# Seven products of halves inside the real part: the product P2 of two blocks of a Strassen kernel made as inner products

## The chip, the cores and the metric

The kernel runs on one core of one Trainium2 chip. The time is the device time of one execution in microseconds; the kernel before takes 701.67 us in the median of three runs (701.47 to 701.92). Five engines run beside each other: TensorE (PE, with its weight loads PEld), VectorE (DVE), ScalarE (ACT), GpSimd (POOL) and SyncE (SP). Here the last two only issue DMAs: SP the loads, POOL the stores and the DMAs that add to their destination.

## The reference

Inputs are x (2048 x 512), DFT matrices over the sequence (2048 x 2048, real and imaginary) and over the hidden axis (512 x 512, the same), the weights w1, w3 (512 x 1376) and w2 (1376 x 512), and a gate vector (512). What is computed:

```
g = sigmoid((x * gate_w).sum(-1))
a = x @ dft_hid_re.T ;  b = x @ dft_hid_im.T
A = dft_seq_re @ a - dft_seq_im @ b
h = silu(x @ w1) * (x @ w3)
out = g * A + (1 - g) * (h @ w2)
```

All is float32. The kernel reaches that precision by splitting each operand into a rounded high part and the rest, a low part, and making three matmuls of each product: high by high, high by low, low by high.

## The kernel before, in words

The work comes in three stages on TensorE. First the hidden DFT (tiles dP), whose results a and b go to DRAM (`ab`). Then gate and up (tiles X, Y, Z), eleven chunks of 128 columns, whose product h goes to DRAM (`hsp`). Then six blocks of large products, each with 512 output rows and 1024 columns: `BLOCKS` numbers them b = 0 to 5, with m = 0 for h @ w2 (b 0, 1), m = 1 for the real part (b 2, 3) and m = 2 for the imaginary part (b 4, 5). j = 0 or 1 is the half of the 2048 columns.

Each block is one product of 2 x 2 submatrices made in Strassen's way (Winograd's form) as seven products P1 to P7. The stationary operand comes from `ab` or w2 in forms of A11, A12, A21, A22; the moving operand from the sequence matrix (`cc`) or h, in forms of B11, B12, B21, B22: F1 = B11+B12, F2 = F1+B22, F3 = B12+B22, F4 = F2+B21. P2 is A12 x B21.

**Steps.** `STEPS` is the list of all work of TensorE in this stage, in order; `AT` gives the place of a step. One step is one product with one quarter of the inner dimension: 12 matmuls of 128x512. `step(n)` makes the matmuls, then calls `advance(n)`, then the tasks hung at that step (`TASKS`), and, where a product is complete, takes the result out of PSUM. `advance(n)` loads the raw blocks of steps up to 8 ahead (`load_c`, tiles B), sums the form of the step 4 ahead (`sum_c`, line 658, on VectorE) and splits that of the step 3 ahead (`split_c` through `split`, lines 71 and 74: ScalarE makes the high part zh, VectorE the low part zl). These tiles stand in a pool of 8 (`zo`), four steps' worth.

**Forms of A.** The stationary forms are made ahead. `forms(m, q, ks, keep)` loads the rows of one quarter and makes the products' forms `ks` in place in the order given by `IN_PLACE` (`sum_a`, lines 481 to 488), splits each (lines 71, 74) and either stores it to DRAM (`fsp`, line 514) or keeps it (`keep`). It returns a list of pieces. The pieces of gate and up are put into one list, `later`, and `work(count)` takes some from it at hooks h0 to h4 of each chunk (`item`). Kept forms are made as tasks during the blocks. `load_a` loads stored ones back (tiles a0, a1, a2). Kept and loaded forms share 28 buffers (`op`). Raw blocks, weights of gate and up (`load_w`, line 249), raw rows, forms under way to DRAM and results share 19 buffers (`f4`).

**Inner products.** In the imaginary part P2 of both blocks is not made in steps of its own. Both have the same A12; so their two B21 together are one product of 2 x 2 submatrices, of half the size, and it too is made as seven products. These are the steps whose names begin with L: `inner_step` puts two half steps of 6 matmuls each for every inner product between the outer steps (`BETWEEN` says after which), `inner(n)` runs them in one PSUM tile (Lx), line 831 adds each inner result to the result tile that P1 began, and the inner stationary forms come from `inner_forms` by way of DRAM (`lsp`, `load_inner`, tiles fl and al). The raw inner blocks are tiles LB. In these blocks F4 and two of the inner forms are not summed on VectorE: `add_block` (line 646) issues a DMA on POOL's queue that reads the second block and adds it to the tile in SBUF, behind the split that has read the tile. Block 2 has one such sum too, F3 (`BY_DMA`).

**What sets the order.** The program is written with a framework that places the waits, gives out buffers and orders each engine's instructions by a cost model of its own; loads by `fetch` and the instructions marked `pinned` keep the written order. SP's and POOL's queues issue in order: a load that waits for a buffer holds the loads behind it.

In the diff `LB` holds the blocks with inner products and `INTO` where each inner result goes. `finish` (lines 767 to 797) ends a quarter of a block: for m = 1 it scales and adds only two quarters of block 3 and stores the others as they are (`ysp`); for m = 2 it subtracts, scales and adds to the output.

Of the kernel before, what the change touches and what calls it, by code (L numbers as in the profile page):

```python
# [7 lines left out]
F32 = mybir.dt.float32  # L8
# [4 lines left out]
P = 128  # L13
# [5 lines left out]
NP = (NC - 1) // 2  # L19
NQ = 4  # L20
WARM = 16


HEAD = ((0, 0, 0, 256), ("d", 0, 0, 512), (0, 0, 256, 256), (1, 0, 0, 512), ("d", 1, 0, 512),
# [4 lines left out]
def fnet_swiglu_gate_kernel(  # L29
# [29 lines left out]
    def raw(name, n=1024):  # L59
        return f4.tile([P, n], F32, tag="f4", name=name)  # L60
# [414 lines left out]
    A = {}  # L475
# [54 lines left out]

    def inner_forms():

        st = {}

        def cols(t, v):
            return t.rearrange("p (c h e) -> p c h e", c=4, h=2)[:, :, v]

        def quads(ap):
            return ap.rearrange("p (c e) -> p c e", c=4)

        def load():
            for h in range(2):
                st[h] = raw(f"rl{h}")
                for q in range(2):
                    nc.sync.dma_start(
                        st[h][:, q * 512 : (q + 1) * 512], ab[1, 1, 2 * h + q, :, 0].rearrange("p i e -> p (i e)"))

            st["a11"], st["a21"], st["a12"], st["a22"] = (cols(st[h], v) for h in range(2) for v in range(2))

        def total(k):  # L550
            st[k] = sum_a(st, k)

        def parts(k):
            src = st[k]
            t = f4.tile([P, 2, 512], F32R, tag="f4", name=f"fl{k}")
            split(quads(t[:, 0]), quads(t[:, 1]), src)
            nc.gpsimd.dma_start(lsp[PRODS.index(k)], flat(t.bitcast(F32)))
# [26 lines left out]
    todo = list(INNER)  # L584
# [7 lines left out]
    count, BETWEEN = 0, (4, 5, 7, 8, 10, 11, 13, 14, 17, 19)  # L592
    LORDER = ("P1", "P5", "P6", "P7", "P3", "P4")
    for b, (m, j) in enumerate(BLOCKS):
        for k, form in ((k, FORM[k]) for k in LORDER) if b in LB else CHAIN:
            for q in range(NQS[m]):
                AT[b, k, q] = len(STEPS)
                STEPS.append((b, k, q, form))
                if len(todo) <= 12:
                    if count in BETWEEN:  # L600
                        inner_step()
                    count += 1
            if b in LB and k == "P6":

                for _ in range(2):
                    inner_step()
# [38 lines left out]
    def add_block(t, b, k, q):  # L645
        nc.gpsimd.dma_start(half(t, chunks(b, q)), block(b, k, q), accum_op=ALU.add)

    BY_DMA = (2,)

    def sum_c(n):  # L650
        if not 0 <= n < len(STEPS):
            return
        b, k, q, form = STEPS[n]
        o = {"F1": "B12", "F2": "B22", "F4": "B21", "F3": "B22", "LF2": "LB22", "LF3": "LB22"}.get(form)
        if not o or q == "pl" or form == "F3" and b in BY_DMA or form == "F4" and b in LB:
            return
        t = RAW[b, "L" * (form[0] == "L") + ("B12" if form[-2:] == "F3" else "B11"), q]
        nc.vector.tensor_add(t, t, RAW[b, o, q])  # L658

    def split_c(n):  # L660
        if not 0 <= n < len(STEPS):
            return
        b, k, q, form = STEPS[n]
        if q == "pl":
            r = PL[b]
            if form == "n1" and k == "P3":
                t = zo.tile([P, 1024], F32R, tag="zo", name=f"zp{n}")
                split(t[:, :512], t[:, 512:], r["n1"])
                r["z"] = t
            elif form == "n1":  # L670
# [10 lines left out]
        f3 = "B22" if b in BY_DMA else "B12"  # L681
        inner = form[0] == "L"
        blk = form[1:] if inner else form
        src = RAW[b, "L" * inner + {"F1": "B11", "F2": "B11", "F4": "B11", "F3": f3}.get(blk, blk), q]
# [121 lines left out]
    def inner(n):  # L806
        b, k, h, form = STEPS[n]
        k = k[1:]
        if h == 0:
            if not LPS:  # L810
                z = pair(3, "Lx")
                LPS.update(P1=z[:, 0], P5=z[:, 1], P2=z[:, 1])
        ps = LPS[{"P6": "P1", "P7": "P1", "P4": "P1", "P3": "P5"}.get(k, k)]
        w = A["L", k]
        zh, zl = ZO.pop(n)
        for i in range(2):
            c = slice(i * 512, (i + 1) * 512)
# [5 lines left out]
        if h == 1:  # L823
            r, g = INTO[k]
            if k == "P1":
                U["P1", LB[1]] = half(raw("uL"))
            t = U["P1", LB[1 - g]]
            if k == "P1":
                nc.scalar.activation(t[:, r], ps, AF.Copy)
            else:  # L830
                (nc.vector.tensor_sub if g else nc.vector.tensor_add)(t[:, r], t[:, r], ps)
            if k in ("P7", "P2"):
                finish(LB[1 - g], 0, 0, t)

    def step(n):
        b, k, q, form = STEPS[n]
        m, j = BLOCKS[b]
        if k[0] == "L":
            if q == 0 and k in ("LP7", "LP2"):
                load_other(LB[k == "LP2"], 0, 0)  # L840
            return inner(n)
        end = b == len(BLOCKS) - 1
        if q == 0:
# [100 lines left out]
    later += inner_forms()  # L944

    def work(count):
        for _ in range(count):
# [24 lines left out]
    for c in range(NC):  # L972
# [59 lines left out]
        act(b, "P1", lambda b=b: load_gate(b))  # L1032
    start = AT[2, "P1", 0]
    for q in range(NQ):
        for i, f in enumerate(forms(1, q, ("P7", "P2", "P4"), True)):
            TASKS.setdefault(start + 3 * q + max(i - 1, 0), []).append(f)
    for i, (k, q) in enumerate(A0[8:]):
        TASKS.setdefault(int(1.25 * i), []).append(lambda k=k, q=q: load_a(0, k, q))
# [11 lines left out]
        TASKS.setdefault(AT[3, "P1", 0] + 1 + 7 * i // 4, []).append(f)  # L1050
    for k, h in INNER:
        if not h:
            TASKS.setdefault(AT["L", k, 0] - 8, []).append(lambda k=k: load_inner(k))
    def gated(q):

        t = half(RAW[LB[1], "B11", q])
        tc.keep_in_program_order(nc.vector.tensor_mul(t, t, twice(GT[LB[1]], 0)))

    for q in (2, 3):
        TASKS.setdefault(AT[LB[1], "P3", q - 2], []).append(lambda q=q: gated(q))  # L1060
    for n in range(len(STEPS)):
        step(n)

# [60 lines left out]
```

## Time and profile before

| | |
|---|---|
| median of 3 runs | 701.67 us |
| profiled execution | 701.09 us, span 699.3 us |
| TensorE granted clock | 1.00 |
| gate and up on TensorE | about 81 to 287 us |
| blocks 0 and 1 (h @ w2) | about 287 to 393 us |
| blocks 2 and 3 (real part) | about 393 to 546 us |
| blocks 4 and 5 (imaginary part) | about 546 to 696 us |

The page gives each engine's busy time and share of the span. The chain of waits goes back from the last instruction to what released it at each step, here told in order of time. The rows by stage give the busy time of PE, PEld, DVE, ACT and POOL, then the granted clock, the share in which the 16 DMA engines were busy, and GB/s. The rows of groups name line, engine, operation, output and input tiles, shape and count, then busy time, mean ns of one and the idle time before.

### The profile page before, as it was taken

The page shows a single profiled execution, that of the slowest core. Times are in us where ns is not written, and L with a number is a line of the kernel's source. Part 1 is how long each engine was busy: PE and PEld are TensorE (multiplying, and loading weights), DVE is VectorE, ACT ScalarE, POOL GpSimd, SP SyncE. Part 2 cuts the span into 40 slices and gives each one's busy share as a digit, 9 for nine tenths or more (in the row PEclk, how much of TensorE's full clock was granted, in tenths as well). Part 3 has the DMA queues.
Part 4 walks back from the last instruction along what each step waited for, and adds up shares of the span by engine and source line. Part 5 has one row for each costly group of instructions (what it writes and reads, how often), then busy time and mean ns, then how long its engine had stood idle before and what let it go on. Part 6 is the DMA issues. An engine that isn't in the chain of part 4 may idle for free.

```text
span 699.3 us, 8634 instructions
## 1 busy us (share of the span) xinstructions
PE 694.6 (99%) x3061; PEld 573.4 (82%) x3061; DVE 577.3 (83%) x646; ACT 356.5 (51%) x417; POOL 85.5 (12%) x136
## 2 busy tenths in 40 slices
PE   9999999999999999999999999999999999999997
PEld 7888888888888888888888888888888888888886
DVE  5999577786879896869998897679785976999886
ACT  6746255555556554474463475446534444544531
POOL 0012212221222220000000001000000020111110
PEclk9999999999999999999999999999999999999999
DMA  8489925785777989697598959720989979798923
GB/s 300 139 289 317 369 94 222 272 286 210 255 289 268 361 311 409 236 347 245 184 330 314 329 196 214 276 112 31 342 295 361 354 133 290 210 352 244 215 32 90
DMA packets 54604, 177.01 MB, mean 253 GB/s; under 512 B 5852, under 2 KB 6620, under 8 KB 54560
## 3 DMA queue, kind: packets, MB, share of 16 engines
q1 hardware_dynamic: 35312, 109.98, 45.1%
q0 software_dynamic: 19104, 66.34, 29.6%
q8 instruction: 24, 0.39, 0.2%
q14 instruction: 20, 0.16, 0.1%
q10 hardware_dynamic: 144, 0.13, 0.1%
HBM read 117.96 MB, written 58.47 MB: 252 GB/s over the span
## 4 chain that ended last, share of the span: by engine, by line
PE 95%; DVE 2%; DMA 1%; SPq 1%; issue 0%; ACT 0%; DVEq 0%; ACTq 0%
PE P L81 55%; PE X L81 17%; PE Z L81 9%; PE dP L81 7%; PE Lx L81 3%; PE Yi L81 2%; PE Y L81 1%; DMA xB<-xt 1%; PE last L81 1%; SPq L109 0%; DVE dt0P L230 0%; DVE xF L142 0%; DVE xF L145 0%; DVE dv L159 0%; DVE xB L151 0%
## 5 line engine op out<-in xcount | busy, mean ns | idle before, releaser
L71 ACT ACTIVATE zh<-B 128x1024 fp32r<-128x1024 f32 (+1 forms) x142 | 146.0, 1031 | 168.8 <-PE P L81 135.7
L74 DVE TENSOR_TENSOR zl<-B,zh 128x1024 fp32r<-128x1024 f32 (+1 forms) x142 | 166.9, 1182 | 47.5 <-ACT zh L71 41.3
L81 PE MATMUL P<-zh,f1P 128*128 128x512 f32 x320 | 99.8, 389 | 0.0
L81 PE MATMUL P<-zh,a2P 128*128 128x512 f32 x280 | 89.0, 389 | 0.0
L81 PE MATMUL P<-zh,a0P 128*128 128x512 f32 x280 | 87.4, 389 | 0.0
L658 DVE TENSOR_TENSOR B<-B,B 128x1024 f32<-128x1024 f32 (+1 forms) x70 | 83.4, 1202 | 0.4
L81 PEld LDWEIGHTS P<-zh,f1P 128*128 128x128 f32 x320 | 60.1, 188 | 12.6
L81 PE MATMUL P<-zl,f1P 128*128 128x512 f32 x160 | 62.2, 389 | 0.0
L81 PEld LDWEIGHTS P<-zh,a2P 128*128 128x128 f32 x280 | 52.5, 188 | 10.9
L81 PEld LDWEIGHTS P<-zh,a0P 128*128 128x128 f32 x280 | 52.6, 188 | 10.9
L81 PE MATMUL P<-zl,a0P 128*128 128x512 f32 x140 | 54.5, 389 | 0.0
L81 PE MATMUL P<-zl,a2P 128*128 128x512 f32 x140 | 54.5, 389 | 0.0
L81 PE MATMUL P<-zh,a1P 128*128 128x512 f32 x128 | 40.7, 389 | 0.0
L81 PEld LDWEIGHTS P<-zl,f1P 128*128 128x128 f32 x160 | 30.0, 188 | 6.1
L81 PEld LDWEIGHTS P<-zl,a0P 128*128 128x128 f32 x140 | 26.3, 188 | 5.5
L81 PEld LDWEIGHTS P<-zl,a2P 128*128 128x128 f32 x140 | 26.3, 188 | 5.4
L81 PE MATMUL P<-zh,f2P 128*128 128x512 f32 x88 | 28.9, 389 | 0.0
L81 PEld LDWEIGHTS P<-zh,a1P 128*128 128x128 f32 x128 | 24.0, 188 | 5.0
L71 ACT ACTIVATE zh<-LB 128x1024 fp32r<-128x1024 f32 x14 | 14.9, 1063 | 20.4 <-PE P L81 18.9
L81 PE MATMUL P<-zl,a1P 128*128 128x512 f32 x64 | 24.9, 389 | 0.0
L74 DVE TENSOR_TENSOR f2P<-r,f2P 128x512 fp32r<-128x512 f32 x24 | 16.1, 682 | 7.1 <-ACT f2P L71 7.1
L74 DVE TENSOR_TENSOR zl<-LB,zh 128x1024 fp32r<-128x1024 f32 x14 | 17.1, 1219 | 4.4 <-ACT zh L71 4.4
(1073 smaller groups left out, 1472.6 us busy)
## 6 DMA issues: line engine op xcount, KB each, us to landing
B<-cc SPq DMA_DIRECT2D x56, 512.0 KB, 5.7
r<-ab SPq DMA_DIRECT2D x24, 512.0 KB, 6.2
hsp<-u POOLq DMA_DIRECT2D x18, 512.0 KB, 5.5
fsp<-f2P POOLq DMA_DIRECT2D x18, 512.0 KB, 4.5
a2P<-fsp SPq DMA_DIRECT2D x18, 512.0 KB, 7.5
B<-hsp SPq DMA_DIRECT2D x16, 512.0 KB, 4.9
fsp<-f0P POOLq DMA_DIRECT2D x14, 512.0 KB, 4.2
a0P<-fsp SPq DMA_DIRECT2D x14, 512.0 KB, 8.1
```

The lines of the kernel that those rows point to most:

```text
L71: i = nc.scalar.activation(hi, src, AF.Copy)
L74: nc.vector.tensor_sub(lo, src, hi.bitcast(F32))
L81: nc.tensor.matmul(ps, u, v, start=first and n == 0, stop=last and n == 2, skip_group_check=chain)
L658: nc.vector.tensor_add(t, t, RAW[b, o, q])
```

## The change

The real part's blocks 2 and 3 are treated as blocks 4 and 5 are. Their P2 becomes seven inner products, placed in the same pattern, so their products run in the order P1, P5, P6, P7, P3, P4; their F4 is added by DMA, and F3 of block 2, which was, is summed on VectorE again. The first copy of P1, which went from PSUM to PSUM for P2 to add to, goes to a result tile in SBUF.

The inner forms of the real part are one more group of seven pieces in gate and up; the four P2 forms that were kept are no longer made. In gate and up the load of each group of forms is no piece of its own any more: it is hung onto the piece that stands two places ahead of the group's first (`EARLY`). The third hook of odd chunks takes no piece. All in all 63 pieces take the place of 65.

```diff
-    lsp = dram.tile([len(PRODS), P, 1024], F32, tag="lsp", name="lsp")
+    lsp = dram.tile([2, len(PRODS), P, 1024], F32, tag="lsp", name="lsp")
...
         def one(i):
             if i < 0:
-                load()
-                total(ks[0])
-            else:
-                parts(ks[i])
+                return load()
+            if i == 0:
+                for k in ks[:2]:
+                    total(k)
+            parts(ks[i])
             if i + 2 < len(ks):
                 total(ks[i + 2])
...
-    def inner_forms():
+    def inner_forms(m):
...
-                        st[h][:, q * 512 : (q + 1) * 512], ab[1, 1, 2 * h + q, :, 0].rearrange("p i e -> p (i e)"))
+                        st[h][:, q * 512 : (q + 1) * 512], ab[m - 1, 1, 2 * h + q, :, 0].rearrange("p i e -> p (i e)"))
...
-    def load_inner(k):
-        t = A["L", k] = op.tile([P, 2, 4, P], F32R, tag="op", name=f"al{k}")
-        fetch(t.bitcast(F32).rearrange("p v c e -> p (v c e)"), lsp[PRODS.index(k)])
+    def load_inner(m, k):
+        t = A[m, "L" + k] = op.tile([P, 2, 4, P], F32R, tag="op", name=f"al{m}{k}")
+        fetch(t.bitcast(F32).rearrange("p v c e -> p (v c e)"), lsp[m - 1, PRODS.index(k)])
...
-    LB = (4, 5)
+    LB = {b: (b - b % 2, b - b % 2 + 1) for b in range(2, 6)}
...
-    def inner_step():
+    def inner_step(b):
         k, h = todo.pop(0)
-        AT["L", k, h] = len(STEPS)
-        STEPS.append((LB[1], "L" + k, h, "L" + FORM[k]))
+        AT[b, "L" + k, h] = len(STEPS)
+        STEPS.append((b, "L" + k, h, "L" + FORM[k]))
...
     for b, (m, j) in enumerate(BLOCKS):
+        if b in LB and b == LB[b][0]:
+            todo, count = list(INNER), 0
         for k, form in ((k, FORM[k]) for k in LORDER) if b in LB else CHAIN:
...
-                if len(todo) <= 12:
+                if b in LB and len(todo) <= 12:
                     if count in BETWEEN:
-                        inner_step()
+                        inner_step(LB[b][1])
                     count += 1
...
-    LOADS += [(AT["L", k, h] - e, LB[1], "L" + blk, h) for blk, k, e in
+    LOADS += [(AT[b, "L" + k, h] - e, b, "L" + blk, h) for b in (3, 5) for blk, k, e in
...
-    BY_DMA = (2,)
-
...
-        if not o or q == "pl" or form == "F3" and b in BY_DMA or form == "F4" and b in LB:
+        if not o or q == "pl" or form == "F4" and b in LB:
...
-        if form == "B22" and b in BY_DMA:
-            add_block(src, b, "B12", q)
-        elif form == "F2" and b in LB:
+        if form == "F2" and b in LB:
             add_block(src, b, "B21", q)
...
             if k == "P1":
-                U["P1", LB[1]] = half(raw("uL"))
-            t = U["P1", LB[1 - g]]
+                U["P1", b] = half(raw(f"uL{b}"))
+            t = U["P1", b - g]
...
-    later = []
-    for q in range(NQS[0]):
-        later += forms(0, q, IN_PLACE, False)
-    early = len(later)
-    later += prep_w2l()
-    for q in range(3):
-        later += forms(2, q, [k for k in IN_PLACE if k != "P2"], False)
-    for q in range(2):
-        later += forms(1, q, ("P1", "P5", "P6", "P3"), False)
-    later += inner_forms()
+    groups = [forms(0, q, IN_PLACE, False) for q in range(NQS[0])] + [prep_w2l()]
+    groups += [forms(2, q, [k for k in IN_PLACE if k != "P2"], False) for q in range(3)]
+    groups += [forms(1, q, ("P1", "P5", "P6", "P3"), False) for q in range(2)]
+    groups += [inner_forms(m) for m in (2, 1)]
+
+    later = groups[0]
+    for g in groups[1:]:
+        n = max(len(later) - EARLY, 0)
+        later[n] = lambda f=later[n], load=g[0]: (f(), load())
+        later += g[1:]
...
         def h2(c=c):
-            work(1)
+            work(1-(c%2))
...
-        for i, f in enumerate(forms(1, q, ("P7", "P2", "P4"), True)):
+        for i, f in enumerate(forms(1, q, ("P7", "P4"), True)):
...
-            TASKS.setdefault(AT["L", k, 0] - 8, []).append(lambda k=k: load_inner(k))
+            for m in (1, 2):
+                TASKS.setdefault(AT[2 * m + 1, "L" + k, 0] - 8, []).append(lambda m=m, k=k: load_inner(m, k))
```

`EARLY` is 2. The remaining lines of the diff carry the block number or m through `inner`, `step` and `gated`.

More of the change, by code (lines that the diff above doesn't have):

```diff
@@ L21 @@
 WARM = 16
+EARLY = 2
 HEAD = ((0, 0, 0, 256), ("d", 0, 0, 512), (0, 0, 256, 256), (1, 0, 0, 512), ("d", 1, 0, 512),
@@ L542, in load @@
             for h in range(2):
-                st[h] = raw(f"rl{h}")
+                st[h] = raw(f"rl{m}{h}")
                 for q in range(2):
                     nc.sync.dma_start(
-                        st[h][:, q * 512 : (q + 1) * 512], ab[1, 1, 2 * h + q, :, 0].rearrange("p i e -> p (i e)"))
+                        st[h][:, q * 512 : (q + 1) * 512], ab[m - 1, 1, 2 * h + q, :, 0].rearrange("p i e -> p (i e)"))
             st["a11"], st["a21"], st["a12"], st["a22"] = (cols(st[h], v) for h in range(2) for v in range(2))
@@ L554, in parts @@
             src = st[k]
-            t = f4.tile([P, 2, 512], F32R, tag="f4", name=f"fl{k}")
+            t = f4.tile([P, 2, 512], F32R, tag="f4", name=f"fl{m}{k}")
             split(quads(t[:, 0]), quads(t[:, 1]), src)
-            nc.gpsimd.dma_start(lsp[PRODS.index(k)], flat(t.bitcast(F32)))
+            nc.gpsimd.dma_start(lsp[m - 1, PRODS.index(k)], flat(t.bitcast(F32)))
         return ahead(load, total, parts, IN_PLACE)
-    def load_inner(k):
-        t = A["L", k] = op.tile([P, 2, 4, P], F32R, tag="op", name=f"al{k}")
-        fetch(t.bitcast(F32).rearrange("p v c e -> p (v c e)"), lsp[PRODS.index(k)])
+    def load_inner(m, k):
+        t = A[m, "L" + k] = op.tile([P, 2, 4, P], F32R, tag="op", name=f"al{m}{k}")
+        fetch(t.bitcast(F32).rearrange("p v c e -> p (v c e)"), lsp[m - 1, PRODS.index(k)])
     def fetch(o, i):
@@ L578, in fnet_swiglu_gate_kernel @@
     PLAIN = {"P3": "n1", "P7": "n1", "P2": "n0", "P4": "n01"}
[L581 removed]
+    LB = {b: (b - b % 2, b - b % 2 + 1) for b in range(2, 6)}
     FORM = dict(CHAIN)
     INNER = [(k, h) for k in ("P1", "P5", "P6", "P3", "P7", "P4", "P2") for h in range(2)]
[L584 removed]
+    todo = []
     STEPS, AT = [], {}
[L587 removed]
+    def inner_step(b):
         k, h = todo.pop(0)
[L589 to L592 removed]
+        AT[b, "L" + k, h] = len(STEPS)
+        STEPS.append((b, "L" + k, h, "L" + FORM[k]))
+    BETWEEN = (4, 5, 7, 8, 10, 11, 13, 14, 17, 19)
     LORDER = ("P1", "P5", "P6", "P7", "P3", "P4")
     for b, (m, j) in enumerate(BLOCKS):
+        if b in LB and b == LB[b][0]:
+            todo, count = list(INNER), 0
         for k, form in ((k, FORM[k]) for k in LORDER) if b in LB else CHAIN:
@@ L680, in split_c @@
         w = chunks(b, q) * 512
-        f3 = "B22" if b in BY_DMA else "B12"
         inner = form[0] == "L"
         blk = form[1:] if inner else form
-        src = RAW[b, "L" * inner + {"F1": "B11", "F2": "B11", "F4": "B11", "F3": f3}.get(blk, blk), q]
+        src = RAW[b, "L" * inner + {"F1": "B11", "F2": "B11", "F4": "B11", "F3": "B12"}.get(blk, blk), q]
         h, l = (zo.tile([P, w], F32R, tag="zo", name=f"z{v}{n}") for v in "hl")
@@ L808, in inner @@
         k = k[1:]
[L809 to L812, printed above, removed]
+        if h == 0 and k == "P1":
+            z = pair(3, f"Lx{b}")
+            LPS.update(P1=z[:, 0], P5=z[:, 1], P2=z[:, 1])
         ps = LPS[{"P6": "P1", "P7": "P1", "P4": "P1", "P3": "P5"}.get(k, k)]
-        w = A["L", k]
+        w = A[BLOCKS[b][0], "L" + k]
         zh, zl = ZO.pop(n)
@@ L1052, in fnet_swiglu_gate_kernel @@
         if not h:
-            TASKS.setdefault(AT["L", k, 0] - 8, []).append(lambda k=k: load_inner(k))
+            for m in (1, 2):
+                TASKS.setdefault(AT[2 * m + 1, "L" + k, 0] - 8, []).append(lambda m=m, k=k: load_inner(m, k))
     def gated(q):
-        t = half(RAW[LB[1], "B11", q])
-        tc.keep_in_program_order(nc.vector.tensor_mul(t, t, twice(GT[LB[1]], 0)))
+        t = half(RAW[5, "B11", q])
+        tc.keep_in_program_order(nc.vector.tensor_mul(t, t, twice(GT[5], 0)))
     for q in (2, 3):
-        TASKS.setdefault(AT[LB[1], "P3", q - 2], []).append(lambda q=q: gated(q))
+        TASKS.setdefault(AT[5, "P3", q - 2], []).append(lambda q=q: gated(q))
     for n in range(len(STEPS)):
```

6 lines of the change are left out of this document (3 added, 3 removed).

## The prediction

> **What bounds the kernel now.** I read the first lines of the page, then the chain of waits in order of time, then what TensorE waited for, then the busy time by stage.
>
> ```profile
> span 699.3 us, 8634 instructions
> PE 694.6 (99%) x3061; PEld 573.4 (82%) x3061; DVE 577.3 (83%) x646; ACT 356.5 (51%) x417; POOL 85.5 (12%) x136
> ```
>
> ```profile
> 228.36 2.72 PE X L81 x12
> ...
> 244.00 5.44 PE X L81 x24
> 249.44 2.72 PE Z L81 x12
> 252.16 5.44 PE X L81 x24
> ...
> 287.52 291.04 PE P L81 x1284
> 578.56 2.72 PE Lx L81 x12
> 581.28 13.60 PE P L81 x60
> 594.88 1.36 PE Lx L81 x6
> 596.24 2.72 PE P L81 x12
> 598.96 1.36 PE Lx L81 x6
> 600.32 5.44 PE P L81 x24
> ```
>
> ```profile
> PE wps L917 <- PEq L1114: 0.8, 1, 0.8
> ```
>
> The second fence is the chain: start, length, engine and tile, matmuls. From 287.52 us it is TensorE alone: 1284 matmuls in 291.04 us, 0.2267 us each, and every later piece begins where the one before ended. The third is the only line of TensorE's own waits. So each matmul taken away shortens the kernel by 0.2267 us, as long as the others keep it fed. Who feeds it shows in the stages (columns: PE, PEld, DVE, ACT, POOL busy, clock, DMA share, GB/s):
>
> ```profile
> 393.40:545.80 152.40, 152.40 (x674) 126.17 (x674) 123.69 (x119) 76.00 (x83) 7.82 (x12) 1.00 0.70 239
> 545.80:695.50 149.70, 149.70 (x661) 123.65 (x659) 130.33 (x117) 67.63 (x66) 18.93 (x20) 1.00 0.77 212
> 81.20:287.40 206.20, 206.20 (x911) 170.38 (x910) 158.46 (x225) 108.66 (x147) 39.64 (x67) 1.00 0.75 276
> ```
>
> The first row is the real part (blocks 2 and 3), which the change rewrites; the second the imaginary part, which has the inner products already; the third gate and up. The granted clock is 1.00 throughout. VectorE is next after TensorE: 81% in the real part, 87% in the imaginary part.
>
> **The change part by part.**
>
> *TensorE.* P2 of blocks 2 and 3 goes: 2 x 4 steps of 12 matmuls (one such step is the 2.72 us row at 596.24), 96 matmuls. Seven inner products of two half steps come, 6 matmuls each (the 1.36 us row at 594.88): 84. The other six products are only reordered. So 12 matmuls less: 12 x 0.2267 = 2.72 us, which is what the two stages above show between them (152.4 against 149.7). This lies wholly on the chain.
>
> *VectorE in the real part.* The rows are of that stage, then of the imaginary part, by form: count, busy time, mean ns.
>
> ```profile
> L74 DVE TENSOR_TENSOR zl<-B,zh 128x1024 fp32r<-128x1024 f32 x57 | 69.4, 1221 | 27.2 <-ACT zh L71 27.1
> L658 DVE TENSOR_TENSOR B<-B,B 128x1024 f32<-128x1024 f32 x29 | 35.1, 1219 | 0.3
> L74 DVE TENSOR_TENSOR f1P<-r,f1P 128x512 fp32r<-128x512 f32 x12 | 7.8, 683 | 0.0
> ```
>
> ```profile
> L831 DVE TENSOR_TENSOR uP<-uP,Lx 128x512 f32<-128x512 f32 x4 | 2.7, 676 | 0.0
> ```
>
> 56 splits become 62: +6 x 1.22 = +7.3 us. Sums: eight F4 go (B21 is added by DMA), four F3 of block 2 come back from the DMA, four inner sums come: no change. Four form splits of P2 go: -4 x 0.68 = -2.7. Six inner results and half of one P1 are added out of PSUM: +7 x 0.68 = +4.7. Together +9.3 us, so 133.0 of 149.7 us, 89%. The imaginary part runs at 130.3 of 149.7 with TensorE never waiting, so it is the nearest witness, 2.7 us lighter.
>
> Where the cover is thinnest there:
>
> ```profile
> 597.88 2.35 DVE L74 TENSOR_TENSOR zl<-B,zh 128x1024 fp32r<-128x1024 f32 x2
> ```
>
> The first of these two splits (done about 599.1) is for the step that TensorE starts at 600.32: 1.2 us ahead, the least in that stage. Three finishing operations of block 4 stood before it; in the real part that product finishes with one, the rest goes out by DMA, so the same place is easier. What the real part has more is forms: two per quarter in block 2's first 12 steps, six of the imaginary part's last quarter early in block 3. The row above also gives the pitch of back-to-back splits: 2.35 - 1.22 = 1.13 us. The fullest stretch is block 3's first 12 outer and 6 inner steps, TensorE 32.6 + 8.2 = 40.8 us. VectorE has there 18 splits and 10 sums, 4 half-size results, 6 form splits and 4 form sums: at pitch 28 x 1.13 + 14 x 0.59 = 39.9 us, at full duration 28 x 1.22 + 14 x 0.68 = 43.7. Between keeping up and falling 2.9 us behind; I take the pitch, since a busy VectorE runs at it, and charge nothing. What covers it is the lead of the splits, 3 steps; if that were gone, each us behind would be a us lost.
>
> *ScalarE in the real part.* Six more 1.06 us splits, four form copies, two P2 copies and two PSUM copies less, three smaller copies more: about +2 us on 76.0. It has half the stage free: nothing. The first copy of P1 now goes to a tile in SBUF instead of PSUM; the sums over it come later than before, and nothing waits for them but a store.
>
> *DMA in the real part.*
>
> ```profile
> 545.80:621.90 76.10, 76.10 (x337) 63.02 (x336) 64.23 (x57) 36.94 (x37) 9.86 (x11) 1.00 0.87 246
> ```
>
> ```profile
> alP<-lsp SPq DMA_DIRECT2D x7, 512.0 KB, 8.3
> ```
>
> Eight B21 loads are exchanged for eight loads of inner blocks. Seven inner forms are loaded more on SP's queue, each 8 steps ahead: some 14 us even where inner steps are among them, against 8.3 us to land. Twelve adding DMAs take the place of four on POOL's. From the stage's row, 0.70 x 152.4 us for 239 GB/s x 152.4 us is 1.54 us of all engines per 512 KB; seven loads and eight adds, an add counted once or twice, are 23 to 35 us: share 0.87 to 0.95 of 149.7 us. Block 4 (the row above) stands 0.87 without a wait of TensorE: I charge nothing; the upper end is rival 3. Each add waits on POOL for its split; behind it stand only stores of results, whose buffers come free that much later.
>
> *Gate and up.* The second inner group adds 7 splits and 4 sums of half size, no load pieces remain, the odd chunks have one slot less.
>
> ```profile
> L74 DVE TENSOR_TENSOR flP<-rl,flP x7: 679/684/691, 245.6 to 261.9; 128x512 fp32r<-128x512 f32 x7
> ```
>
> ```profile
> 249.48 1.22 DVE L439 TENSOR_TENSOR u<-u,X 128x1024 f32<-128x1024 f32 x1 [0.30 <-PE X L81]
> ```
>
> That is 11 x 0.68 = 7.5 us of VectorE on 158.5 of 206.2 us: 80%. The tight place is line 439: it must read X before TensorE comes back to X at 252.16, and ends at 250.70, 1.46 us ahead. One half-size operation in front of it (0.68) fits, three do not. At worst six even chunks each lose 3 x 0.68 - 1.46 = 0.6 us, 3.5 us; at best nothing. Those pieces stand in front of it already and no wait shows, so I take nothing. Loads two pieces ahead take away waits of ScalarE that TensorE never felt: nothing gained, nothing lost, but for the buffers (second rival).
>
> *Sum.* The profiled execution took 701.09 us, 0.58 below the median; with 2.72 less it is 698.4. On the median, 701.67 - 2.72 = **698.95 us**, 0.39% less; about 0.2% (1.4 us) is what a measurement of this kernel can tell from no change.
>
> **The rivals.**
>
> *1. VectorE falls behind in block 3.* With the 2.9 us of the upper bound and a lead not full when block 3 begins, the gain is eaten: 698.95 + 2.9 = 701.9; half of it, 700.4. For: 89% busy, and two dense stretches. Against: ScalarE's splits mostly wait for TensorE to free their tiles, that is, the lead is full:
>
> ```profile
> ACT zh L71 <- PE P L81: 159.6, 107, 3.0
> ```
>
> *2. Slower: the early loads of forms take the buffers of the weights in gate and up.* Every group's two raw tiles now come two pieces sooner: with 63 pieces over about 206.2 us that is 2 x 3.3 = 6.5 us, out of the 19 buffers that the weights use as well.
>
> ```profile
> SPq L249 <- DMA fsp<-f0P: 49.2, 4, 22.4
> ```
>
> ```profile
> 220.63 0.33 SPq L249 DMA_DIRECT2D ws<-w  x1
> ```
>
> ```profile
> DMA to landing us min/median/max: 3.1/4.7/7.1
> ```
>
> ```profile
> 226.24 0.63 ACT L71 ACTIVATE wa<-ws 128x512 fp32r<-128x512 f32 x1
> ```
>
> Weight loads (line 249) wait for a buffer already, up to 22.4 us. This one lands at about 220.63 + 4.7 = 225.3, and ScalarE splits it at 226.24, 0.9 us later. If it slips, ScalarE stands in its queue, behind it the 0.6 us copy that TensorE needs when the X piece at 228.36 ends, 231.08. The stall is slip + 225.3 + 0.63 + 0.6 - 231.08, slip less 4.5 us. With one group's 6.5 us that is 2.0 and no change remains (700.9); from a slip of 8.6 us the kernel is slower than measurement noise; with two groups ahead of it, 13 us, it is 8.5: 707.5. Against: TensorE has no wait in gate and up although the waits of 249 are long.
>
> *3. The adding DMAs land late.*
>
> ```profile
> L646 POOL DMA_DIRECT2D B<-cc x12: 842/859/922, 421.3 to 652.4; - x12
> ```
>
> ```profile
> 572.93 0.85 POOL L646 DMA_DIRECT2D LB<-cc  x1 [1.79 <-DVE zl L74]
> ```
>
> ```profile
> 586.53 1.06 ACT L71 ACTIVATE zh<-LB 128x1024 fp32r<-128x1024 f32 x1 [1.66 <-PE P L81]
> ```
>
> ```profile
> DMA to landing us min/median/max: 5.4/6.6/9.7
> ```
>
> The first inner add is issued at 572.93 and its sum is split at 586.53: 13.6 us against 9.7 at most, 3.9 us to spare. Above that by more than the split's lead TensorE waits; I put the loss at about 1 us per block, 701. The same issue takes 842 to 922 ns wherever VectorE is busy or not. In the Trainium skill, "SBUF — State Buffer", section "SBUF: two separate sides", warns that POOL cannot write the descriptors of its DMAs while VectorE holds the port that both share. By that rule each of the eight further adds would be held for up to one VectorE operation, 1.2 us, inside what is to spare; the rows above do not show it even in 646 to 653 us, where VectorE never rests.
>
> *4. The matmul count is not what bounds.* Then nothing changes: 701.7. Against it stand the equal 0.2267 us pitch in every piece of the chain and the 2.7 us between the two stages. In the Trainium skill, "Perfetto Trace Analysis", section "Identifying the Most-Contended Engine", says that matmul busy time is a bad measure and weight loading a better one; by its 82% there would be 18% of room and matmuls would not be the price. The chain decides for the pitch here.
>
> **How the numbers follow.** Forecast 0.70, rival 1 0.09, rival 2 0.14, rival 3 0.05, rival 4 0.02. Faster is the forecast, 0.70; slower is rival 2, 0.14; the others are no change, 0.16. The low end is the lowest run, 701.47, less 2.72, less the runs' spread of 0.4: 698.4. The high end takes in rivals 1, 3 and 4 with the spread of the runs, 702.2, which leaves out about 0.15. The forecast's own range is 698.4 to 700.2.
>
> **What would show it.** Right: 1788 matmuls instead of 1800 after gate and up; the real part's stage 149.7 us; VectorE about 133 us in it, DMA share about 0.9; no new line among TensorE's waits. Wrong: gaps in the chain in block 3 with VectorE as releaser (rival 1), in gate and up with ScalarE behind a weight load (rival 2), or at the inner splits with a DMA behind (rival 3); or the same end with fewer matmuls at a longer pitch (rival 4).

## The result, and the profile after

The changed kernel takes 699.07 us in the median of its seven executions (the lowest 698.85), the kernel before 701.27 us in seven on the same chip: a ratio of 0.9967, with 95% from 0.9955 to 0.9979. That is 2.2 us less, where 2.72 us less had been forecast. The first execution of the changed kernel ran at a granted TensorE clock of 0.558 from end to end (1176.47 us) and does not count in the ratio, and the profile shown below is that of a later one at 1.00, which took 699.07 us.

First the head of its page, then its chain of waits in order of time (start, length, engine and tile, matmuls), cut to the pieces that matter:

```profile
span 697.3 us, 8695 instructions
PE 692.2 (99%) x3049; PEld 571.2 (82%) x3049; DVE 591.7 (85%) x666; ACT 362.1 (52%) x425; POOL 96.3 (14%) x151
```

```profile
197.22 2.97 PE X L82 x12
...
287.90 138.72 PE P L82 x612
426.62 2.72 PE Lx L82 x12
429.34 13.60 PE P L82 x60
...
497.34 10.88 PE P L82 x48
...
510.94 65.28 PE P L82 x288
...
687.74 5.45 PE last L82 x24
...
693.64 0.33 DVEq L1119
```

The same pieces of the chain of the kernel before that were not shown yet:

```profile
197.08 2.72 PE X L81 x12
...
690.08 5.45 PE last L81 x24
...
695.98 0.33 DVEq L1120
```

This pair of chains holds the whole account of these two executions. From the first matmul of the six blocks to the last piece it was 690.08 - 287.52 = 402.56 us, and it is 687.74 - 287.90 = 399.84 us: 2.72 us less, to the hundredth what twelve matmuls at 0.2267 us make. Every piece inside begins where the one before ends, and the page counts 3049 matmuls for 3061. But the span is only 699.3 - 697.3 = 2.0 us shorter. 0.38 us is lost ahead of the blocks (they start at 287.90 instead of 287.52), of which 0.25 us is the longer piece at 197.22, and 0.3 us behind them: the last entry of VectorE's queue ends 3.0 us before the end of the span in the kernel before (696.31 to 699.3) and 3.3 us in the changed one (693.97 to 697.3).

TensorE's own waits have the one line that they had. Below it are the stages, gate and up, real part, imaginary part, with the columns as before (PE, PEld, DVE, ACT, POOL busy, clock, DMA share, GB/s):

```profile
PE wps L915 <- PEq L1113: 0.8, 1, 0.8
```

```profile
81.40:287.80 206.40, 206.40 (x911) 170.30 (x910) 164.00 (x234) 111.19 (x153) 42.93 (x73) 1.00 0.81 292
393.90:543.40 149.50, 149.50 (x661) 123.80 (x660) 130.96 (x128) 78.19 (x84) 14.78 (x20) 1.00 0.87 288
543.40:692.80 149.40, 149.40 (x661) 123.69 (x659) 130.56 (x117) 67.69 (x66) 18.91 (x20) 1.00 0.78 220
```

The real part is now as long as the imaginary part. No wait of TensorE appeared, yet the work beside it has moved closer at three places. They are read here, since the experiments are about them.

**Block 2, before P7.** ScalarE's and VectorE's instructions in order of time (start, length, what, and in brackets how long the engine had been idle and what ended it):

```profile
425.29 0.63 ACT L72 ACTIVATE f1P<-r 128x512 fp32r<-128x512 f32 x1 [2.28 <-DMA r<-ab]
425.83 2.00 ACT L72 ACTIVATE zh<-B 128x1024 fp32r<-128x1024 f32 x2
427.73 1.00 ACT L897 ACTIVATE uP<-P 128x1024 f32<-128x1024 f32 x1
```

```profile
427.70 1.22 DVE L75 TENSOR_TENSOR zl<-B,zh 128x1024 fp32r<-128x1024 f32 x1
```

ScalarE stands idle for 2.28 us until raw rows of a kept form have landed. Behind that in its queue stand two splits and the copy that empties a PSUM tile (line 897). VectorE's part of the first split ends at 428.92, the copy at 428.73, and TensorE starts P7 at 429.34 (chain): 0.4 us to spare. The loads of these rows from 394 us on, first of the kernel before, then of the changed one (count, duration in ns, first and last issue), and SP's wait ahead of them in the changed kernel (total, times, longest):

```profile
L499 SPq DMA_DIRECT2D r<-ab x3: 319/319/383, 393.8 to 397.8; - x3
```

```profile
L500 SPq DMA_DIRECT2D r<-ab x4: 319/351/383, 403.4 to 418.9; - x4
```

```profile
SPq L500 <- DVE f1P L75: 14.2, 2, 7.6
```

The last such load was issued at 397.8 us; now SP waits for a buffer until the split of an earlier form is done (`f1P`, line 75), and the load is issued at 418.9.

**Block 3, P5 and P6.** One of VectorE's splits, and the row of busy times over 28 us:

```profile
498.01 1.22 DVE L75 TENSOR_TENSOR zl<-B,zh 128x1024 fp32r<-128x1024 f32 x1
```

```profile
483.00:511.00 28.00, 28.00 (x125) 23.18 (x124) 28.00 (x30) 16.87 (x19) 3.98 (x5) 1.00 0.83 256
```

VectorE is busy for 28.00 of 28.00 us. The split, done at 499.23, is for the second step of P6, which TensorE starts at 497.34 + 2.72 = 500.06: 0.8 us ahead.

**Gate and up, at the longer piece.** ScalarE, then VectorE:

```profile
194.60 0.63 ACT L72 ACTIVATE f1P<-r 128x512 fp32r<-128x512 f32 x1 [2.35 <-DMA hsp<-u]
```

```profile
195.27 0.69 DVE L75 TENSOR_TENSOR f1P<-r,f1P 128x512 fp32r<-128x512 f32 x1 [1.28 <-ACT f1P L72]
195.88 1.21 DVE L440 TENSOR_TENSOR u<-u,X 128x1024 f32<-128x1024 f32 x1
```

ScalarE waits 2.35 us for a buffer that a store of h must free. VectorE stands behind it, and its addition of X (now line 440) ends at 197.09, just too late for TensorE's return to X. In the kernel before the addition began at 193.72.

### The profile page after: what moved, and what is told of

The parts are those of the page before. It is cut to its first block, busy times and chain, and to the rows that moved or that the text cites. A ratio compares the mean times of both kernels' runs of the same rounds, so it can differ in the third digit from the quotient of the medians.

```text
span 1174.7 us, 8695 instructions
## 1 busy us (share of the span) xinstructions
PE 1169.7 (100%) x3049; PEld 665.0 (57%) x3049; DVE 605.3 (52%) x666; ACT 364.7 (31%) x425; POOL 96.1 (8%) x151
## 4 chain that ended last, share of the span: by engine, by line
PE 100%; DVE 0%; DVEq 0%; issue 0%
PE P L82 52%; PE X L82 17%; PE dP L82 10%; PE Z L82 9%; PE Lx L82 5%; PE Yi L82 2%; PE Y L82 1%; PE dP L206 1%; PE last L82 1%; PE wps L915 0%; DVE uP L795 0%; DVEq L1119 0%
## 5 line engine op out<-in xcount | busy, mean ns | idle before, releaser
L82 PE MATMUL P<-zh,a2P 128*128 128x512 f32 x280 | 137.5, 576 | 0.0
L82 PE MATMUL P<-zh,a0P 128*128 128x512 f32 x280 | 135.9, 577 | 0.0
L82 PE MATMUL P<-zh,f1P 128*128 128x512 f32 x256 | 125.9, 577 | 0.0
L82 PE MATMUL P<-zl,a0P 128*128 128x512 f32 x140 | 80.4, 574 | 0.0
L82 PE MATMUL P<-zl,a2P 128*128 128x512 f32 x140 | 80.4, 574 | 0.0
L75 DVE TENSOR_TENSOR zl<-LB,zh 128x1024 fp32r<-128x1024 f32 x28 | 34.3, 1225 | 59.5 <-ACT zh L72 59.5
L82 PE MATMUL P<-zh,a1P 128*128 128x512 f32 x128 | 62.9, 574 | 0.0
L72 ACT ACTIVATE zh<-LB 128x1024 fp32r<-128x1024 f32 x28 | 29.6, 1059 | 90.3 <-PE P L82 85.8
L82 PE MATMUL P<-zh,f2P 128*128 128x512 f32 x88 | 45.1, 582 | 0.0
L82 PEld LDWEIGHTS P<-zl,a0P 128*128 128x128 f32 x140 | 30.7, 219 | 23.0 <-issue 12.9
L440 DVE TENSOR_TENSOR u<-u,X 128x1024 f32<-128x1024 f32 x11 | 13.4, 1221 | 32.0 <-PE X L82 22.3
```

The costliest lines, as they stand in the source:

```text
L72: i = nc.scalar.activation(hi, src, AF.Copy)
L75: nc.vector.tensor_sub(lo, src, hi.bitcast(F32))
L82: nc.tensor.matmul(ps, u, v, start=first and n == 0, stop=last and n == 2, skip_group_check=chain)
L440: nc.vector.tensor_add(u4, u4, flat(x))
```

## The experiments

My theory was the one predicted: the matmul count sets the time, and the work of the other engines that the change adds hides behind TensorE. The rivals were that the early loads do the work or the harm, that VectorE in block 3 has no room left, and that the pool of buffers has none. Ratios are against the kernel before on the same chip, with 95%.

**The changed kernel beside its experiments.** No edit.

> The changed kernel itself, for a profile at full clock and a closer time. Theory A (only the matmul count matters): 2.72 us less than before, ratio 0.9961, no gap on TensorE after 32.5 us, real part's stage 149.7 us. Theory B (VectorE falls behind in block 3 by a part of a microsecond): 2.2 us less, ratio 0.9969, with gaps in the chain in block 3. Theory C (ScalarE or VectorE late in gate and up): also 2.2 us less, but the gaps stand before 287 us.

Measured: 699.53 us, 0.9977 (0.9964 to 0.9990). The views above are of this run. They bear out theory A in the blocks, and theory C by 0.25 us at the piece at 197.22; block 3 has no gap. With the first comparison, the gain lies between about 1.5 and 2.5 us where both intervals hold, so probably somewhat less than 2.72.

**The early loads alone, on the kernel before.**

```diff
 def one(i):
     if i < 0:
-        load()
-        total(ks[0])
-    else:
-        parts(ks[i])
+        return load()
+    if i == 0:
+        for k in ks[:2]:
+            total(k)
+    parts(ks[i])
...
+    for g in groups[1:]:
+        n = max(len(later) - 2, 0)
+        later[n] = lambda f=later[n], load=g[0]: (f(), load())
+        later += g[1:]
...
-            work(1)
+            work(1-(c%2))
```

> The kernel before with the early loads of forms alone (56 pieces, no inner products in the real part). Theory A: ratio 1.000, within 0.3 us of before. Rival 2: slower than before by 0.5 us or more.

Measured: 701.80 us, 1.0011 (1.0002 to 1.0020): 0.5 us slower by the medians, 0.1 to 1.4 us by the interval. ScalarE's wait and two pieces of the chain in its profile:

```profile
ACT f1P L71 <- DMA hsp<-u: 2.5, 1, 2.5
```

```profile
195.99 1.22 DVE u L439
...
197.26 3.04 PE X L81 x12
```

The addition of line 439 is the link ahead of TensorE here. The stall at 197 us comes from this part of the change, not from the inner products. It is of the second rival's kind, a buffer of the shared pool that is not free, but what waits is a tile for a form and not one for a weight, and the price in this chain is 0.3 us (3.04 for 2.72) instead of 2. It is not there in every execution: the run with sixteen matmuls less below has the same gate and up as the changed kernel and loses 0.2 us at another X piece, at 177.5 us.

**The inner products with each group's load as a piece of its own.**

```diff
     for g in groups[1:]:
-        n = max(len(later) - EARLY, 0)
-        later[n] = lambda f=later[n], load=g[0]: (f(), load())
-        later += g[1:]
+        later += g
...
-            work(1-(c%2))
+            work(1)
```

> The changed kernel with each group's load of forms as a piece of its own again, right before the group, and the third hook of odd chunks taking a piece. Theory A: the time of e1 within 0.3 us, because TensorE felt no wait of ScalarE for a load. Rival 2 (early loads take buffers from the weights): up to 0.6 us faster than e1. If the early loads are what makes room for the second inner group: slower than e1 by 1 us or more, with gaps in gate and up.

Measured: 700.12 us, 0.9982 (0.9973 to 0.9990). By the medians that is 0.6 us above the changed kernel, which fits none of the three outcomes expected, but the two intervals overlap almost wholly, so it is not to be told from it. The gain therefore comes from the inner products. TensorE's waits in its profile, which was of a run of 701.59 us:

```profile
PE P L82 <- ACT uP L897: 0.9, 1, 0.9
...
PE P L82 <- ACT g L456: 0.6, 1, 0.6
```

The wait at 197 us is gone and two others are there: one at the end of gate and up, and one at the thin place of block 2, where the copy behind ScalarE's wait came too late this time. The same wait stands in the profiles of two further versions below, the one with sixteen matmuls less and the one with forms later, at 0.2 us each. So that place does cost time in some executions.

**Sixteen matmuls less in block 3.** In P6 one of the three terms is left out.

```diff
-    def mm3(ps, ah, al, bh, bl, first, last, chain=False):
-        for n, (u, v) in enumerate(((ah, bh), (ah, bl), (al, bh))):
+    def mm3(ps, ah, al, bh, bl, first, last, chain=False, terms=3):
+        for n, (u, v) in enumerate(((ah, bh), (ah, bl), (al, bh))[:terms]):
...
-                            (own and qq == 0 or len(todo) == 2 and qq == todo[0][0]) and i == 0, (qq == NQS[m] - 1 or n == len(STEPS) - 3) and i == nch - 1, True)
+                            (own and qq == 0 or len(todo) == 2 and qq == todo[0][0]) and i == 0, (qq == NQS[m] - 1 or n == len(STEPS) - 3) and i == nch - 1, True, 2 if b == 3 and k == "P6" else 3)
```

> The changed kernel with the low-by-high matmul left out of P6 of block 3 (16 matmuls less, in the densest stretch of VectorE; that part of the product is not computed). Theory A with room on VectorE: 16 x 0.2267 = 3.63 us less than e1. Theory B (VectorE is the limit there already): the time of e1, or a gain of less than 2 us.

Measured: 698.28 us, 0.9952 (0.9938 to 0.9965). 16 x 0.2267 = 3.63 us were taken away; 1.25 us came back by the medians, 1.8 by the two ratios. Its waits of TensorE and its chain through block 3:

```profile
PE P L82 <- DVE zl L75: 0.6, 1, 0.6
PE P L82 <- ACT uP L897: 0.2, 1, 0.2
```

```profile
481.48 8.18 PE P L82 x36
...
508.15 1.22 DVE zl L75
509.42 65.39 PE P L82 x287
```

Between 489.7 and 509.4 us the chain is VectorE's, not TensorE's. From the first matmul of the blocks (287.89) to the last piece (686.33) it is 398.44 us, so sixteen matmuls took 1.40 us off the 399.84 and 2.2 us were lost: about 1.7 in and right behind block 3's dense stretch (its 81 matmuls from 489.66 to 509.42 take 19.76 us, for 18.4 at pitch), the rest at block 2's P7. Here, then, the matmul count is no longer the price: VectorE bounds block 3 as soon as TensorE asks for more.

**VectorE's work doubled at four steps of block 3.** The low part of P5's splits is made twice, some 4.5 us of VectorE.

```diff
         split(h, l, src)
+        if b == 3 and k == "P5":
+            nc.vector.tensor_sub(l, src, h.bitcast(F32))
```

> The changed kernel with VectorE's split made twice in the four P5 steps of block 3 (the second writes the same values): 4 x 1.13 = 4.5 us more of VectorE. Theory V: the splits stand 0.7 us ahead at the thinnest place, so about 3.8 us come out as gaps in block 3, 3 to 4 us above e1. With room on VectorE: the time of e1.

Measured: 703.61 us, 1.0032 (1.0020 to 1.0044), about 4 us more than the changed kernel (4.1 by the medians), as expected. In the chain of its profile the blocks take 403.33 us (288.95 to 692.28), 3.5 us more than 399.84, so most of the addition comes out as time there; the rest of the difference stands ahead of the blocks.

```profile
PE P L82 <- DVE zl L689: 2.5, 2, 1.7
```

The two runs bound the room from both sides: little for less matmul time, little for more VectorE time. In the kernel as changed the two are level to within about 1 us.

**Six forms of the imaginary part made later in block 3.** This takes them out of the full 28 us.

```diff
-        TASKS.setdefault(AT[3, "P1", 0] + 1 + 7 * i // 4, []).append(f)
+        TASKS.setdefault(AT[3, "P3", 0] + i if i < 6 else AT[3, "P1", 0] + 1 + 7 * i // 4, []).append(f)
```

> The changed kernel with the six kept forms of the imaginary part's last quarter made at block 3's P3 and P4 instead of during its P1 and P5. Theory V (VectorE has just enough room in block 3, its splits there done 0.7 to 1.9 us ahead of TensorE): the splits of P6 in block 3 stand 3 us or more ahead; the time is that of e1 or up to 0.5 us less, since only some executions lose something there. Theory A (nothing but the matmul count): the same time as e1.

Measured: 699.52 us, 0.9977 (0.9968 to 0.9985). No gain by itself, which fits: block 3 shows no wait in the changed kernel's profile. But VectorE has room now, with 23.72 us busy from 483 to 511 us.

**The rows of block 2's kept forms out of the way.** P7 and P4 of two quarters are made in gate and up too and only loaded in block 2.

```diff
-    groups += [forms(1, q, ("P1", "P5", "P6", "P3"), False) for q in range(2)]
+    groups += [forms(1, q, [k for k in IN_PLACE if k != "P2"], False) for q in range(2)]
...
-    for q in range(NQ):
+    for q in (2, 3):
...
+    for i, (k, q) in enumerate((k, q) for k in ("P7", "P4") for q in range(2)):
+        TASKS.setdefault(start + 4 + 2 * i, []).append(lambda k=k, q=q: load_a(1, k, q))
```

> The changed kernel with the P7 and P4 forms of the real part's quarters 0 and 1 made in gate and up and loaded back, so that block 2 loads raw rows for two quarters instead of four. Theory R (ScalarE stands in its queue for the raw rows of the last quarter, 2.3 us in e1's profile, 3.7 in e2's, and the splits of block 2's P7 come out 0.3 us ahead or late): that wait goes, the P7 splits stand 2 us or more ahead, no gap near 430 us, the median 0.3 to 1 us less than e1 and its runs closer together. If four more pieces in gate and up crowd it: gaps before 287 us and no gain.

Measured: 699.89 us, 0.9981 (0.9971 to 0.9991). ScalarE's 2.28 us wait for `r` is gone from its profile and so is the long piece at 197; the time is not to be told from the changed kernel's. The 0.3 to 1 us expected did not come.

**Both, and both again.** The last two edits together, measured twice.

> Both edits of e5 and e6. Theories V and R together: the whole 2.72 us, ratio 0.9961 against before, about 698.5, with runs closer together than those of e1. If the loss of e1 is elsewhere (gate and up, the tail): the time of e1.

> e7 once more, beside runs of the kernel before on this chip. If the two waits found are all that the changed kernel lost: ratio 0.9961 to 0.9970 and no run above 700.5.

Measured: 699.08 us, 0.9969 (0.9957 to 0.9981), and 699.56 us, 0.9975 (0.9965 to 0.9985). That is no measured gain over the changed kernel: the whole 2.72 us that I expected missed, and the second time also the range of 0.9961 to 0.9970. So these two places are not what the medians lack. In the profiles of both, as in that of the changed kernel, the blocks take 399.84 us; they begin at 287.12 us in the first and at 287.86 in the second, so 0.7 us of start can differ between two executions of one kernel. But the same 28 us of block 3, which come about 1 us earlier in the first of these, now read:

```profile
482.00:510.00 28.00, 28.00 (x126) 23.17 (x124) 23.29 (x22) 14.77 (x15) 3.96 (x5) 1.00 0.89 249
```

VectorE has 4.7 us free where it had none. Whether that is worth anything, the next run tells.

**Both, and sixteen matmuls less.** The edit of P6 on top of these two; the same term is left out.

> e7 with the low-by-high matmul left out of P6 of block 3, as in e4 (that part of the product is not computed). Theory V: 16 matmuls less are now worth their full 3.63 us against e7, where e4 gained about 1.3 against e1. If VectorE is the bound over all of block 3 whatever the forms do: less than 2.5 us.

Measured: 695.40 us, 0.9918 (0.9905 to 0.9930), 3.68 us less than the first measurement of the version with both edits and 4.2 less than the second, for 3.63 us of matmuls.

```profile
PE wps L915 <- PEq L1115: 0.8, 1, 0.8
```

```profile
288.09 138.72 PE P L82 x612
...
497.53 7.25 PE P L82 x32
...
684.30 5.45 PE last L82 x24
```

The chain is free of that noise: 684.30 - 288.09 = 396.21 us for the blocks, 3.63 us less than 399.84. The same cut that gave 1.40 us in the chain before gives its full price now, with no wait of TensorE, and the piece that holds P6 is 32 matmuls in 7.25 us, 0.2267 us each. So VectorE's place in block 3 withheld most of it and block 2's P7 the rest; the cut with only one of the two edits was not measured.

**One buffer less in the pool of 19, on the changed kernel and on the kernel before.**

```diff
-    f4 = ctx.enter_context(tc.tile_pool(name="f4", bufs=19, side="right"))
+    f4 = ctx.enter_context(tc.tile_pool(name="f4", bufs=18, side="right"))
```

> The changed kernel with 18 instead of 19 buffers in the shared pool. Theory R (in block 2 the raw rows of the last quarter wait for a buffer of this pool, and ScalarE for them): the load goes out later, ScalarE's wait for r grows beyond 3 us, gaps of 1 us or more before block 2's P7, 1 to 3 us above e1. If the buffers are not what it waits for: the time of e1.

> The control: the kernel before with 18 buffers. If the change used up the pool's reserve: the kernel before changes by less than 0.5 us. If the pool is short in either kernel: it loses as much as e9 loses.

Measured: the changed kernel 707.14 us, 1.0083 (1.0070 to 1.0096); the kernel before 702.16 us, 1.0012 (1.0003 to 1.0021). One buffer is worth 7.6 us after the change by the medians and 7.4 by the ratios, well above the 1 to 3 us expected, and 0.7 to 0.8 us before it, a little more than the 0.5 that I had allowed. TensorE's waits in the first, ScalarE's entry ahead of the longest of them, then TensorE's wait in the second:

```profile
PE P L82 <- ACT uP L897: 4.0, 1, 4.0
PE Yi L82 <- DVE s L394: 1.3, 1, 1.3
PE P L82 <- DVE zl L75: 1.0, 1, 1.0
```

```profile
430.70 0.63 ACT L72 ACTIVATE f1P<-r 128x512 fp32r<-128x512 f32 x1 [3.06 <-DMA r<-ab]
```

```profile
PE P L81 <- DVE zl L74: 0.8, 1, 0.8
```

The longest wait is block 2's thin place again, now torn open. So the change has used up the pool's reserve. What took it is argued from the program, not shown: P1's copy lies in a tile of it, the loads of forms take theirs earlier, and seven more forms pass through it. How much each of these takes was not separated.

## Why the prediction was right, and where a size was off

**The sum.** Twelve matmuls less at 0.2267 us, wholly on the chain, was right in mechanism and to 0.01 us in size between the first matmul of the blocks and the last piece. The forecast of 698.95 us stands against medians of 699.07 and 699.53. That the first is so close is in part luck: I subtracted from 701.67, the median of three executions, and the kernel before has 701.27 in all seven, so a base that was 0.4 us too high hid a gain that was 0.5 us too large. What the sum lacks are two terms: about 0.3 us in gate and up, which I had set to nothing, and 0.3 us at the end, which I did not have. Together with 0.1 us of start, which also differs between executions of one kernel, these turn 2.72 into the 2.0 of the profile.

**VectorE in the real part.** I forecast +9.3 us, 133.0; the stage's row has 130.96, 7.3 more. The groups of that stage say why (count, busy time, mean ns):

```profile
L75 DVE TENSOR_TENSOR zl<-B,zh 128x1024 fp32r<-128x1024 f32 x49 | 59.2, 1218 | 9.3 <-ACT zh L72 9.2
L75 DVE TENSOR_TENSOR zl<-LB,zh 128x1024 fp32r<-128x1024 f32 x14 | 17.1, 1219 | 4.7 <-ACT zh L72 4.7
L75 DVE TENSOR_TENSOR f1P<-r,f1P 128x512 fp32r<-128x512 f32 x8 | 5.2, 681 | 1.9 <-ACT f1P L72 1.9
```

The counts are as worked out: 49 + 14 = 63 splits for 57, eight `f1P` for twelve. The stage has 128 instructions for 119, and 6 - 4 + 7 = 9. The durations of all groups of the stage add up to 130.3 us before and 139.5 after, 9.2 more, so the forecast was right as a sum of durations. But neighbours overlap, 1.13 us from start to start for 1.22 us of duration, and a stage's busy time counts the overlap once; the more of them stand back to back, the less each adds. That the stage has 88% was no guide to its tightest 28 us, which have 100%.

**Rival 1, VectorE in block 3 (0.09).** It did not come about, and the choice of 39.9 us at pitch over 43.7 at full duration was right: in the 40.8 us from 467.42 to 508.22 VectorE makes 42 operations, as many as I had counted, and is busy for 39.50. But it was close to the edge, with 0.8 us of lead left. The runs with fewer matmuls and with more VectorE work show that the condition was right and that the changed kernel stands about 1 us short of the point from which it decides. No run tests the bound of 2.9 us.

**Gate and up.** VectorE +5.5 us for 7.5 forecast, for the same reason. I named line 439 as the tight place and charged nothing, since the pieces ahead of it had done no harm. It was the place: but what came in front of it was not one piece more; it was one that stood waiting for ScalarE. Cost 0.25 us, inside the 0 to 3.5 that I had given.

**Rival 2, early loads and buffers (0.14).** The shortage of buffers is there, shown by the early loads alone (1.0011), but at a price of 0.3 to 0.5 us. No wait of TensorE behind a weight load appeared. With one buffer less the loss is 7.4 to 7.6 us, most of it in block 2, which I had not named; that this is near the 8.5 us of my upper case, worked out for weights in gate and up, is chance. Of block 2 the prediction said that VectorE has two forms per quarter more in the first 12 steps and that ScalarE has half the stage free. The stage's average was right (78.19 of 149.5, forecast 78) and hid that ScalarE stands in order behind one late load.

**Rival 3, adding DMAs (0.05).** Landing of these DMAs, minimum, median and maximum in the changed kernel, and their issue:

```profile
L650 POOL DMA_DIRECT2D B<-cc x16: 844/859/932, 412.6 to 650.0; - x16
...
DMA to landing us min/median/max: 5.4/8.3/12.9
```

They land up to 12.9 us after their issue, against 9.7 before, and TensorE waited for none. The tight place is block 2, which the prediction did not work out: its first inner add is issued at 422.14, lands 10.9 us later, and its sum is split at 434.59, so about 1.5 us are to spare instead of the 3.9 that I had worked out for block 4. The share of the DMA engines in the stage is 0.87, the lower end of 0.87 to 0.95, where an add counts once. The issue takes 844 to 932 ns, against 842 to 922 before, also inside the 28 us in which VectorE never rests, where the four adds take 844 to 873. By the Trainium skill, "SBUF — State Buffer", section "SBUF: two separate sides", POOL cannot write its descriptors while VectorE runs an operation in a mode that takes both of its ports; the prediction left that condition out. No such hold shows in these rows, and whether VectorE's operations here run in such a mode is not shown.

**Rival 4, the matmul count is not the bound (0.02).** For the step from the kernel before to the changed one it is the bound. Weight loading stands at 82% before and after, while sixteen matmuls gave 3.63 us in the chain once VectorE had room. Without that room the share of busy time misled: TensorE stood at 99%, and half to two thirds of the cut brought nothing. The Trainium skill, "Perfetto Trace Analysis", section "Identifying the Most-Contended Engine", says that matmul busy time is not a good measure of how close a kernel is to the roofline (the chip's peak rate) and names the busy share of weight loading instead; here neither share told what a matmul is worth, and the chain did.

## What to carry to other kernels

A matmul is worth its pitch only while the engine that feeds TensorE has room at that very place: look for windows where that engine's busy time equals the window (28.00 of 28.00 us here), and for the lead of the last split before its matmul (0.8 us here), not at the stage's average. An engine that works its queue in order, as ScalarE does in block 2 here, turns one late load into lateness of all that stands behind it, so a load that waits for a buffer belongs ahead of the stage that is tight. And when a change keeps its time but uses more buffers, take one away on both kernels: it shows how much reserve was spent.

## What the runs showed that I had not expected

A long wait of TensorE cost more than itself. With 18 buffers the changed kernel's TensorE stood for 4.0 us before P7 of block 2, in the one profile taken. The busy times by window show what came behind it (after POOL's comes the granted clock):

```profile
429.80:434.20 4.40, 0.42 (x3) 0.01 (x1) 2.58 (x3) 3.50 (x5) 0.00 (x0) 0.96 1.07 268
434.20:437.70 3.50, 3.50 (x9) 2.78 (x10) 3.50 (x4) 2.31 (x3) 0.00 (x0) 0.52 0.99 330
437.70:442.00 4.30, 4.30 (x20) 3.56 (x19) 1.60 (x2) 1.75 (x2) 0.00 (x0) 1.00 1.03 421
```

For 3.5 us the clock was 0.52 and 9 matmuls were made where 15 fit, 1.5 us lost: with the waits of 4.0, 1.3 and 1.0 us that makes 7.8 us, for 7.6 by the medians and 8.1 between the two profiled executions (705.4 - 697.3). The matmul counts decide here, not the clock alone: in this execution the column reads 0.95 to 0.96 from the start up to that wait, yet from 40 to 60 us TensorE makes 90 matmuls, as many as the changed kernel does at 1.00. The Trainium skill, "TensorE: Matmul & The Clock Gate", section "Part 1: The HAM clock gate (the "warmup" mystery)", states half clock after an idle window of about 3.4 us and full clock after as long a busy one; this wait and these 3.5 us agree with it. The shorter waits in the run with VectorE's doubled splits, 1.7 us at most, left it at 1.00:

```profile
476.00:512.00 36.00, 33.53 (x146) 26.68 (x145) 35.58 (x39) 19.15 (x22) 3.98 (x5) 1.00 0.66 211
```

The end of the program grew by 0.3 us behind the same last store. From the last entry of VectorE's queue to the end of the span it is 3.3 to 3.4 us in every version with the inner products of the real part, and 3.0 to 3.1 us in the kernel before, in that with the early loads alone and in that with 18 buffers. What in it does this was not settled.
